# Attention probabilities stored with 128 columns per head and group, so that each weight load begins on a 256-byte boundary of its tile

## The chip, the cores and the metric

The kernel runs on one core of one Trainium2 chip. The metric is the device time of one execution in microseconds (us), as the median of several. TensorE (PE in the profile) multiplies a stationary operand, its weights, by a moving operand that streams through it. Each matmul here has its own weight load, which the profile lists as a separate engine, PEld. DVE is VectorE, ACT is ScalarE, POOL is GpSimd. All profiles quoted here had a granted TensorE clock of 1.00.

## The reference, cut to what matters

The reference has two halves, a state-space layer and a segmented attention with a small memory. The change touches the attention alone.

```python
# 64 segments of 32 rows, 8 memory rows in front; 32 heads of 128; x is 2048 x 1024
h = jnp.concatenate([mem, xs], axis=1)
q, k, v = (jnp.einsum('btd,dhe->bhte', h, W) for W in (Wq, Wk, Wv))   # shortened
scores = jnp.where(mask, jnp.einsum('bhqe,bhke->bhqk', q, k) * scale, -1e9)
p = softmax(scores)
o = jnp.einsum('bhqk,bhke->bhqe', p, v)
o = jnp.einsum('bhte,hed->btd', o, Wo)
mem = o[:, :8]                                   # goes to the next segment
```

## The kernel before

The segments are packed into 22 groups of 96 rows plus 3 memory rows, 99 in all (`GW`). A unit is two groups by two heads, and there are 16 head pairs with 11 units each, so 176 units. For each unit TensorE computes four transposed score blocks (99 columns each), ScalarE takes their exponentials into `b_e`, GpSimd multiplies by a 0/1 mask into `b_m`, and two units later TensorE uses `b_m` as the weights of four matmuls. Their moving operand is the value tile `b_v`. It has 258 columns per group: a column of ones, the values of two heads, and another column of ones, so the row sum comes out with each product.

```python
GX = 96; GW = 99; VW = 258
...
        for i in range(2):
            t = pool.tile([128, NG, VW], BF16, name=f"b_v{i}", bufs=1)
            G.memset(t[GX:128, :, :], 1.0)
            G.memset(t[:, :, 0:1], 1.0)
            G.memset(t[:, :, VW - 1:VW], 1.0)
            self.vb.append(t)
        for i in range(4):
            t = pool.tile([128, 4 * GW + 32], BF16, name=f"b_m{i}", bufs=1)
            G.memset(t[GX:128, :], 0.0)
            G.memset(t[:, 4 * GW:4 * GW + 32], 0.0)
            self.mb.append(t)
...
    def att_front(self, hp, u):                      # scores, exponential, mask
        ...
                PE.matmul(s[:, j * GW:(j + 1) * GW], kt[:, hh, g0:g0 + 128], qt[:, hh, g0:g0 + GW], start=True, stop=True)
        e = self.p3.tile([GW, 4 * GW], BF16, name="b_e", bufs=3)
        k.S.activation(e[:], s[0:GW, 0:4 * GW], ACT.Exp, scale=float(E) ** -0.5, accum_out=...)
        m = self.mb[i % 4]
        k.G.tensor_tensor(v4(m[0:GW, 0:4 * GW]), v4(e[:]), mask[...], ALU.mult)
...
    def att_back(self, hp, u, m):                    # probabilities times values
        vt = self.vb[hp % 2]
        o = k.ps("O")
        for gg in range(2):
            for hh in range(2):
                j = 2 * gg + hh
                cs = slice(hh * 129, hh * 129 + 129)
                PE.matmul(o[:, gg, cs], m[:, j * GW:j * GW + 128], vt[:, 2 * u + gg, cs], start=True, stop=True)
        ...                                          # reciprocal of the row sums, scaling, store
```

In what follows, positions 0 to 3 are the four matmuls of a unit in the order in which they run (j = 0 to 3). In this kernel their weight loads begin 0, 198, 396 and 594 bytes into `b_m`, and their moving operands begin at 0, 258, 516 and 774 bytes of a stretch of `b_v`.

Of the kernel before, what the change touches and what calls it, by code (L numbers as in the profile page):

```python
# [9 lines left out]
BF16 = mybir.dt.bfloat16  # L10
I32 = mybir.dt.int32
ACT = mybir.ActivationFunctionType
ALU = mybir.AluOpType
# [303 lines left out]
class PartB:  # L317
# [201 lines left out]
    def qk_init(self, pool):  # L519
        V, G = self.k.V, self.k.G  # L520
        self.qk = []
        for i in range(2):
            pair = []
            for n in "qk":
                t = pool.tile([128, 2, QW], BF16, name=f"b_{n}{i}", bufs=1)
                V.memset(t[:, :, 64 + NMX:GX], 0.0)
                V.memset(t[:, :, 21 * GW + 64:21 * GW + GX], 0.0)
                V.memset(t[:, :, NG * GW:QW], 0.0)
                pair.append(t)
            self.qk.append(pair)  # L530
        self.vmst = []
        for i in range(2):
            t = pool.tile([128, 4, 128], BF16, name=f"b_vmst{i}", bufs=1)
            V.memset(t[:, :, NM:128], 0.0)
            self.vmst.append(t)
        self.vb, self.mb = [], []
# [4 lines that stand above are left out]
            G.memset(t[:, :, VW - 1:VW], 1.0)  # L541
            self.vb.append(t)
        for i in range(4):
            t = pool.tile([128, 4 * GW + 32], BF16, name=f"b_m{i}", bufs=1)
            G.memset(t[GX:128, :], 0.0)
            G.memset(t[:, 4 * GW:4 * GW + 32], 0.0)
            self.mb.append(t)

    def load_wqk(self, hp):
# [55 lines left out]
    def att_front(self, hp, u):  # L605
        k = self.k; PE = k.PE
        qt, kt = self.qk[hp % 2]
        s = k.ps("S")
        for gg in range(2):
            g0 = (2 * u + gg) * GW  # L610
# [4 lines that stand above are left out]
        i = hp * NU + u  # L615
        k.S.activation(e[:], s[0:GW, 0:4 * GW], ACT.Exp, scale=float(E) ** -0.5, accum_out=self.accE[0:GW, i:i + 1])  # L616
        m = self.mb[i % 4]
        mask = k.maskA if u == 0 else k.maskB
        v4 = lambda t: t.rearrange("p (a b q) -> p a b q", a=2, b=2)
        k.G.tensor_tensor(v4(m[0:GW, 0:4 * GW]), v4(e[:]), mask[0:GW, :, :].unsqueeze(2).to_broadcast([GW, 2, 2, GW]), ALU.mult)  # L620
        return m

    def att_back(self, hp, u, m):
        k = self.k; PE, V = k.PE, k.V
# [3 lines that stand above are left out]
            for hh in range(2):  # L628
                j = 2 * gg + hh
                cs = slice(hh * 129, hh * 129 + 129)  # L630
                PE.matmul(o[:, gg, cs], m[:, j * GW:j * GW + 128], vt[:, 2 * u + gg, cs], start=True, stop=True)  # L631
        i = hp * NU + u
        r = self.rall[0:GW, 4 * i:4 * i + 4]
        oa = o[0:GW]
        ends = bass.AP(oa.tensor, oa.offset, [list(oa.ap[0]), [512, 2], [257, 2]])
        V.reciprocal(r.rearrange("p (a b) -> p a b", a=2), ends)  # L636
        ot = self.ot[hp]
        V.tensor_tensor(ot[:, 2 * u:2 * u + 2, :].rearrange("p g (h e) -> p g h e", h=2),  # L638
                        oa[:, :, 1:257].rearrange("p g (h e) -> p g h e", h=2),
                        r.rearrange("p (a b) -> p a b", a=2).unsqueeze(3).to_broadcast([GW, 2, 2, E]), ALU.mult)  # L640
        if u == NU - 1:
            os = self.os[hp // 4]
            cs = slice((hp % 4) * 256, (hp % 4) * 256 + 256)
            k.SP.dma_start(os[64:64 + 20 * GX, cs].rearrange("(g p) n -> p g n", p=GX), ot[0:GX, 1:21, :])
            k.SP.dma_start(os[0:64, cs], ot[0:64, 0, :])
            k.SP.dma_start(os[T - 64:T, cs], ot[0:64, 21, :])
            cs = slice(hp * 256, hp * 256 + 256)
            k.SP.dma_start(self.omd[0:NTL, cs].rearrange("(g j) n -> j g n", j=3), ot[GX:GW, :, :])
            k.SP.dma_start(self.omd[NTL:NM, cs], ot[64:64 + NMX, 0, :])
# [489 lines left out]
```

## Time and profile before

| | before |
|---|---|
| time, median of the first 3 runs | 1241.64 us (1241.46 to 1241.79) |
| PE busy, of a span of 1240.4 us | 1230.1 us |
| PE busy in the attention stage, 497 to 1017 us | 519.84 of 520 us |
| weight loads from `b_m`, of all weight loads | 704 of 8148 |

Three lines of the page, kernel before: the busy times by engine, and from the list of groups the matmuls on the probabilities and the largest group of matmuls. The columns of a group are line, engine, operation, output and inputs, shape, count, then busy us with the mean ns of one, then idle time before.

```profile
PE 1230.1 (99%) x8078; PEld 654.6 (53%) x8148; DVE 610.7 (49%) x1124; ACT 326.0 (26%) x754; POOL 211.6 (17%) x290
...
L587 PE MATMUL psP<-b_xe,w 128*128 128x480 bf16 x2048 | 439.3, 366 | 0.0
...
L631 PE MATMUL psO<-b_v,b_m 128*128 128x129 bf16 x704 | 70.0, 221 | 0.0
```

TensorE is the bound. L631 shows a trap: 70.0 us over 704 matmuls are 99 ns each, which for 129 columns looks far too long. But a matmul's end is modelled in this profile, and the recorded time of one (221 ns) reaches well over the start of the next. What a matmul costs in a stream is the time from its start to the next start, here called its pitch. Starts are in the timeline, here of TensorE's matmuls in one unit of the kernel before (start in us, recorded length, then the group):

```profile
599.76 1.90 PE L570 MATMUL psP<-b_xe,w 128*128 128x201 bf16 x20
601.49 0.34 PE L613 MATMUL psS<-b_q,b_k 128*128 128x99 bf16 x4
601.67 0.40 PE L631 MATMUL psO<-b_v,b_m 128*128 128x129 bf16 x4
601.91 1.38 PE L587 MATMUL psP<-b_xe,w 128*128 128x480 bf16 x6
```

The four score matmuls (L613) take from 601.49 to 601.67, which is 45 ns each, and the four on the probabilities (L631) from 601.67 to 601.91, 60 ns each. The starts recorded in the whole trace give means of 56.9, 60.3, 59.3 and 59.4 ns for positions 0 to 3, 58.96 ns over all. (One gap in this trace, of 275 ns, spans a missing record and is left out.)

The view of tile `b_m`, kernel before: each group's count, then minimum, median and maximum ns of one, first and last start.

```profile
L631 PEld LDWEIGHTS <-b_m x704: 97/98/100, 502.3 to 1016.7; 128*128 128x128 bf16 x176
L620 POOL TENSOR_TENSOR b_m<-b_e,maskB x160: 869/871/876, 499.8 to 1015.3; 99x396 bf16<-99x396 bf16 x160
...
  ACT b_e L616: 383.7, 176
```

All 704 loads are recorded at 97 to 100 ns, the aligned ones of position 0 as well as the others. The last line says that GpSimd sat idle for 383.7 us, in 176 waits, for the exponentials. From the end of a unit's multiply to its first load pass 3.8 us in the median, but less in the last head pair: 0.7 us in most of its units, and 0.18 us in the last.

### The profile page before, as it was taken

What the parts mean: (1) busy time and instruction counts of PE and PEld (TensorE: products, weight loads), DVE (VectorE), ACT (ScalarE), POOL (GpSimd) and SP (SyncE); (2) the same over time, 40 slices, a digit from 0 to 9 for tenths busy, and PEclk for the clock granted to TensorE, in tenths of its full rate; (3) what the DMA queues carried; (4) which work ended last, traced back from release to release, by engine and by line L of the source; (5) the groups of instructions that cost most, each with busy time, mean ns of one, the idle gap of its engine ahead of it and who ended that gap; (6) DMA issues with size and microseconds to landing.
All of it is one profiled execution on the core that took longest, in us unless ns stands there. A gap on an engine that the chain in (4) does not pass through costs nothing.

```text
span 1240.4 us, 19648 instructions
## 1 busy us (share of the span) xinstructions
PE 1230.1 (99%) x8078; PEld 654.6 (53%) x8148; DVE 610.7 (49%) x1124; ACT 326.0 (26%) x754; POOL 211.6 (17%) x290
## 2 busy tenths in 40 slices
PE   8999999999999999999999999999999999999998
PEld 4444444444455445566666655655565554454444
DVE  4889999999941122444444444444444550011000
ACT  3344334444310001332333333333333230000000
POOL 2000000000032144222222222232222330000000
PEclk9999999999999999999999999999999999999999
DMA  9942232333666558577668554645575469707000
GB/s 220 261 132 66 87 94 68 102 94 77 153 187 203 154 166 164 106 151 149 134 128 170 124 136 96 128 77 104 106 139 106 73 203 218 153 18 153 17 18 28
DMA packets 306056, 153.95 MB, mean 124 GB/s; under 512 B 147242, under 2 KB 299810, under 8 KB 305962
## 3 DMA queue, kind: packets, MB, share of 16 engines
q1 hardware_dynamic: 304138, 150.82, 52.6%
q10 hardware_dynamic: 1824, 1.84, 0.5%
q8 instruction: 65, 1.06, 0.4%
q14 instruction: 29, 0.24, 0.1%
HBM read 73.70 MB, written 44.71 MB: 95 GB/s over the span
## 4 chain that ended last, share of the span: by engine, by line
PE 98%; DMA 1%; issue 0%; DVE 0%
PE psP L587 33%; PE psS L687 9%; PE psO L256 9%; PE psS L414 9%; PE psP L414 9%; PE psP L687 5%; PE psP L310 4%; PE psS L310 4%; PE psP L570 4%; PE psO L631 3%; PE psS L613 3%; PE psO L687 2%; PE psS L720 1%; PE psP L505 1%; PE psP L739 1%; DMA a_hs<-in_B_Wv_dram 1%
## 5 line engine op out<-in xcount | busy, mean ns | idle before, releaser
L587 PE MATMUL psP<-b_xe,w 128*128 128x480 bf16 x2048 | 439.3, 366 | 0.0
L587 PEld LDWEIGHTS <-w 128*128 128x128 bf16 x2048 | 193.9, 98 | 183.0
L620 POOL TENSOR_TENSOR b_m<-b_e,maskB 99x396 bf16<-99x396 bf16 x160 | 139.4, 871 | 347.5 <-ACT b_e L616 347.5
L77 DVE CAST b_q<-psP 128x480 bf16<-128x480 f32 (+1 forms) x192 | 98.0, 531 | 145.3 <-PE psP L587 133.8
L414 PEld LDWEIGHTS <-b_xe 128*128 128x128 bf16 x1024 | 99.8, 98 | 121.7 <-DMA a_hs<-in_B_Wv_dram 1.1
L75 ACT ACTIVATE b_k<-psP 128x480 bf16<-128x480 f32 x128 | 73.1, 571 | 318.7 <-PE psP L587 318.7
L687 PEld LDWEIGHTS <-b_ol 128*128 128x128 bf16 x960 | 93.1, 98 | 109.3
L616 ACT ACTIVATE b_e<-psS 99x396 bf16<-99x396 f32 x176 | 87.4, 497 | 170.5 <-PE psS L613 161.7
L638 DVE TENSOR_TENSOR b_ot<-psO,b_rall 99x512 bf16<-99x512 f32 x176 | 121.6, 691 | 6.4
L256 PE MATMUL psO<-w,a_bt 128*128 128x512 bf16 x496 | 114.7, 379 | 0.8
L636 DVE RECIPROCAL b_rall<-psO 99x4 f32<-99x4 f32 x176 | 31.1, 177 | 132.5 <-PE psO L631 132.5
L687 PE MATMUL psS<-w,b_ol 128*128 128x512 bf16 x406 | 91.5, 379 | 0.6
L414 PE MATMUL psS<-w,b_xe 128*128 128x512 bf16 x378 | 90.1, 379 | 0.4
L414 PE MATMUL psP<-w,b_xe 128*128 128x512 bf16 x376 | 89.8, 379 | 0.4
L256 PEld LDWEIGHTS <-a_bt 128*128 128x128 bf16 x512 | 49.7, 98 | 59.0
L310 PEld LDWEIGHTS <-a_hs 128*128 128x128 bf16 x512 | 49.5, 98 | 58.3
L77 DVE CAST b_ost<-psS 128x512 bf16<-128x512 f32 x13 | 9.0, 691 | 125.4 <-PE psS L687 125.4
L631 PE MATMUL psO<-b_v,b_m 128*128 128x129 bf16 x704 | 70.0, 221 | 0.0
L613 PEld LDWEIGHTS <-b_k 128*128 128x128 bf16 x704 | 50.0, 98 | 33.9 <-DVE b_k L77 0.2
L613 PE MATMUL psS<-b_q,b_k 128*128 128x99 bf16 x704 | 60.1, 208 | 0.1
L75 ACT ACTIVATE b_vst<-psS 128x512 bf16<-128x512 f32 x56 | 33.4, 597 | 99.1 <-PE psS L414 70.2
L353 POOL MEMSET b_z<- 32x128 bf16 x1 | 0.2, 194 | 341.3 <-DVE a_hs L292 341.3
(205 smaller groups left out, 1162.3 us busy)
## 6 DMA issues: line engine op xcount, KB each, us to landing
b_v<-b_vx SPq DMA_DIRECT2D x16, 1056.0 KB
b_os<-b_ot SPq DMA_DIRECT2D x16, 960.0 KB
w<-in_B_Wv_dram SPq DMA_DIRECT2D x14, 1024.0 KB
b_vx<-b_vst SPq DMA_DIRECT2D x48, 256.0 KB
w<-in_B_Wo_dram SPq DMA_DIRECT2D x12, 1024.0 KB
w<-in_B_Wq_dram SPq DMA_DIRECT2D x16, 512.0 KB
w<-in_B_Wk_dram SPq DMA_DIRECT2D x16, 512.0 KB
a_xn<-in_A_x_dram SPq DMA_DIRECT2D x32, 128.0 KB
```

The costliest lines, as they stand in the source:

```text
L75: self.S.activation(out, in_, ACT.Copy)
L77: self.V.tensor_copy(out, in_)
L256: m = PE.matmul(u[:, i, :], self.bt[:, i, c, :], self.xT[tb][:, c, :], start=(c == 0), stop=(c == KC - 1))
L310: PE.matmul(py[:], self.hs[tb][:, pc, i, tt * 128:(tt + 1) * 128], self.ct[half, i][:, pc, :], start=(pc == 0 and i == 0), stop=(pc == PC ...
L414: m = self.k.PE.matmul(p[:], self.xe[:, c, t * 128:(t + 1) * 128], w[:, c, :], start=(c == 0), stop=(c == KC - 1))
L587: PE.matmul(p[:, 0:480], w[:, i * KC + c, hh * 128:(hh + 1) * 128], self.xe[:, c, 480 * q:480 * q + 480], start=(c == 0), stop=(c == KC - 1))
L613: PE.matmul(s[:, j * GW:(j + 1) * GW], kt[:, hh, g0:g0 + 128], qt[:, hh, g0:g0 + GW], start=True, stop=True)
L616: k.S.activation(e[:], s[0:GW, 0:4 * GW], ACT.Exp, scale=float(E) ** -0.5, accum_out=self.accE[0:GW, i:i + 1])
L620: k.G.tensor_tensor(v4(m[0:GW, 0:4 * GW]), v4(e[:]), mask[0:GW, :, :].unsqueeze(2).to_broadcast([GW, 2, 2, GW]), ALU.mult)
L631: PE.matmul(o[:, gg, cs], m[:, j * GW:j * GW + 128], vt[:, 2 * u + gg, cs], start=True, stop=True)
L638: V.tensor_tensor(ot[:, 2 * u:2 * u + 2, :].rearrange("p g (h e) -> p g h e", h=2), oa[:, :, 1:257].rearrange("p g (h e) -> p g h e", h=2) ...
L687: k.PE.matmul(self.acc[t, half], ol[:, h8, tt * 128:(tt + 1) * 128], self.wo_half(half, h), start=(h == 0), stop=(h == H - 1))
```

## The change

The intent: in the old tile only position 0 loads its weights from the start of the tile, and the other loads begin at odd multiples of 2 bytes and 4 bytes. If a load that begins off a boundary is slower, then 528 loads would gain. The new tile gives each head and group 128 columns (256 bytes). The added columns hold zeros, as the tile is cleared once and only 99 columns of each block are ever written again.

```diff
         for i in range(4):
-            t = pool.tile([128, 4 * GW + 32], BF16, name=f"b_m{i}", bufs=1)
-            G.memset(t[GX:128, :], 0.0)
-            G.memset(t[:, 4 * GW:4 * GW + 32], 0.0)
+            t = pool.tile([128, 4, 128], BF16, name=f"b_m{i}", bufs=1)
+            G.memset(t[:], 0.0)
             self.mb.append(t)
@@ att_front
-        k.G.tensor_tensor(v4(m[0:GW, 0:4 * GW]), v4(e[:]), mask[0:GW, :, :].unsqueeze(2).to_broadcast([GW, 2, 2, GW]), ALU.mult)
+        k.G.tensor_tensor(m[0:GW, :, 0:GW].rearrange("p (a b) q -> p a b q", a=2), v4(e[:]), mask[0:GW, :, :].unsqueeze(2).to_broadcast([GW, 2, 2, GW]), ALU.mult)
@@ att_back
-                PE.matmul(o[:, gg, cs], m[:, j * GW:j * GW + 128], vt[:, 2 * u + gg, cs], start=True, stop=True)
+                PE.matmul(o[:, gg, cs], m[:, j, :], vt[:, 2 * u + gg, cs], start=True, stop=True)
```

The built program keeps the order of all instructions but for four memsets. It places the new tiles 128 bytes past a multiple of 256 (read from the built program), so the boundary is a true one of 128 bytes, and of 256 only within the tile. The changed kernel is one line shorter there, so its L630, L619 and L586 are the L631, L620 and L587 of before.

## The prediction

> What bounds the kernel. TensorE: the page's first part has PE busy 1230.1 of 1240.4 us, and the chain that ended last is 98% PE. In the attention stage (497 to 1017 us) the windows view has PE busy 519.84 of 520 us at a granted clock of 1.00. The change gains only what it takes off PE's own pitch.
>
> What it touches. 704 of 8148 weight loads (those from b_m, four per unit, 176 units) and the GpSimd multiply that writes b_m. The order of instructions on PE, DVE, ACT and SP stays; GpSimd loses four memsets. The old tile's loads begin at 0, 198, 396 and 594 bytes, the new one's at 0, 256, 512, 768. In the built program the new tile begins 128 bytes past a multiple of 256, so loads are aligned to 128 bytes only. Tiles below in the pool move by 640 bytes.
>
> Cost. The group list invites a wrong sum: L631 has 70.0 us for 704 matmuls, 99 ns each, where 129 columns should stream in about 56; 43 ns x 704 would be 30 us. But matmul ends are modelled. Read by starts: in the timeline the four score matmuls start at 601.49, the four b_m matmuls at 601.67, the next projection at 601.91: 45 ns per score matmul (99 columns), 60 per b_m matmul. Over all units, start to start is 44 to 45 ns for L613; for L631 it averages 56.9 after a unit's first matmul, then 60.3, 59.3 and 59 to 60: mean 59.0. The 480-column matmuls have 202.4. A line through 99 and 480 columns gives 56.5 ns at 129 (estimate). All above streaming is thus 2.5 ns x 704 = 1.8 us, 0.14% of the run.
>
> Is even that alignment? I think mostly not. The Trainium skill (TensorE: Matmul & The Clock Gate, Part 2, step 1) says the next weights load while the current matmul runs; the trace agrees: each load starts 2 ns after a matmul starts. The score matmuls load b_k at steps of 198 bytes, just as unaligned, at a pitch of 44 to 45 ns: an unaligned load fits into that and cannot hold up a matmul that streams for 56. A b_m load's record is 97 to 100 ns, aligned or not. The page's section on weight-path perf modes gives as conditions of the fast load 128 weights, not FP32, a bounded column step; no start address. And the slow gaps follow the matmul's own position, also where its successor's weights are aligned; every fourth unit is slow in position 0 too, where only the value operand's address differs. That points to the moving operand (258-byte steps), which stays.
>
> GpSimd. The multiply takes 871 ns; with rows of 99 in a stride of 128 I expect 870 to 950. It idles 384 us waiting for the exponentials, and PE takes b_m about two units (6 us) later: nothing reaches PE.
>
> Prediction: 1241.0 us, range 1239.3 to 1242.4; faster by over 2% 0.01, within 2% 0.98, slower 0.01.
>
> What shows it. Right: L631 starts still about 59 ns apart after positions 1 to 3, loads still 98 ns, PE never waiting for b_m. If alignment mattered, positions 1 to 3 fall to 56 to 57 and the time to about 1239.9. Wrong: a load that costs PE time outside its group, a GpSimd write slow enough to stall PE (over 2.5 us), or the shifted addresses of b_q, b_k, b_v changing other matmuls' pitch.

## The result

| | runs | median us | range us |
|---|---|---|---|
| before | 6 | 1241.76 | 1241.46 to 1242.03 |
| changed | 6 | 1241.76 | 1241.15 to 1242.52 |

The ratio is 1.000, with a 95% interval of 0.9987 to 1.0013: the same. (A ratio is the mean time of one kernel's runs over that of the other's of the same rounds, so not quite the ratio of the medians.)

The same views of the changed kernel: page, timeline of one unit, and tile `b_m`.

```profile
PE 1230.2 (99%) x8078; PEld 654.9 (53%) x8148; DVE 610.8 (49%) x1124; ACT 326.4 (26%) x754; POOL 211.8 (17%) x286
...
L586 PE MATMUL psP<-b_xe,w 128*128 128x480 bf16 x2048 | 439.3, 366 | 0.0
...
L630 PE MATMUL psO<-b_v,b_m 128*128 128x129 bf16 x704 | 69.9, 221 | 0.0
```

```profile
600.78 0.34 PE L612 MATMUL psS<-b_q,b_k 128*128 128x99 bf16 x4
600.97 0.40 PE L630 MATMUL psO<-b_v,b_m 128*128 128x129 bf16 x4
601.20 1.98 PE L586 MATMUL psP<-b_xe,w 128*128 128x480 bf16 x9
```

```profile
L630 PEld LDWEIGHTS <-b_m x704: 96/98/101, 501.6 to 1016.0; 128*128 128x128 bf16 x176
L619 POOL TENSOR_TENSOR b_m<-b_e,maskB x160: 872/874/878, 499.2 to 1014.6; 99x396 bf16<-99x396 bf16 x160
...
  ACT b_e L615: 384.0, 176
```

Nothing that the change aims at has moved. The loads are recorded at 98 ns as before, four matmuls take 0.23 to 0.24 us as before, and the multiply costs 874 ns instead of 871, on an engine that still idles 384 us.

The profiled run of the changed kernel is 0.7 us shorter (1239.7 against 1240.4), and it is worth seeing where. From the start of the span to the first matmul on the probabilities it took 501.69 us against 502.38. From the first of those matmuls to the last it took 514.32 against 514.36. From there to the start of the kernel's last matmul it was 219.85 in both. So the 0.7 us came before the first matmul that the change touches. Two later traces with the aligned tile spent 502.29 and 502.73 us there, so this is scatter from run to run. The middle stretch, called the stretch below, is far more steady than the run time, and is used as the fine measure: four traces, of the kernel before, the changed kernel, a second run of it, and e2_base256 below, have 514.36, 514.32, 514.32 and 514.32 us.

### The profile page after: what moved, and what is told of

Read it like the earlier page. It is cut to its first block, busy times and chain, and to the rows that moved or that the text cites. A ratio compares the mean times of both kernels' runs of the same rounds, so it can differ in the third digit from the quotient of the medians.

```text
span 1239.7 us, 19648 instructions
## 1 busy us (share of the span) xinstructions
PE 1230.2 (99%) x8078; PEld 654.9 (53%) x8148; DVE 610.8 (49%) x1124; ACT 326.4 (26%) x754; POOL 211.8 (17%) x286
## 4 chain that ended last, share of the span: by engine, by line
PE 98%; DMA 1%; issue 0%; DVE 0%
PE psP L586 33%; PE psS L686 9%; PE psO L256 9%; PE psS L414 9%; PE psP L414 9%; PE psP L686 5%; PE psP L310 4%; PE psS L310 4%; PE psP L569 4%; PE psO L630 3%; PE psS L612 3%; PE psO L686 2%; PE psS L719 1%; PE psP L505 1%; PE psP L738 1%; PE psO L482 1%
## 5 line engine op out<-in xcount | busy, mean ns | idle before, releaser
L586 PE MATMUL psP<-b_xe,w 128*128 128x480 bf16 x2048 | 439.3, 366 | 0.0
L586 PEld LDWEIGHTS <-w 128*128 128x128 bf16 x2048 | 193.9, 98 | 183.0
L619 POOL TENSOR_TENSOR b_m<-b_e,maskB 99x396 bf16<-99x396 bf16 x160 | 139.9, 875 | 346.8 <-ACT b_e L615 346.8
L310 PEld LDWEIGHTS <-a_hs 128*128 128x128 bf16 x512 | 49.5, 98 | 58.3
L630 PE MATMUL psO<-b_v,b_m 128*128 128x129 bf16 x704 | 69.9, 221 | 0.0
L612 PE MATMUL psS<-b_q,b_k 128*128 128x99 bf16 x704 | 60.1, 208 | 0.1
```

Source lines behind the costliest of these rows:

```text
L310: PE.matmul(py[:], self.hs[tb][:, pc, i, tt * 128:(tt + 1) * 128], self.ct[half, i][:, pc, :], start=(pc == 0 and i == 0), stop=(pc == PC ...
L586: PE.matmul(p[:, 0:480], w[:, i * KC + c, hh * 128:(hh + 1) * 128], self.xe[:, c, 480 * q:480 * q + 480], start=(c == 0), stop=(c == KC - 1))
L619: k.G.tensor_tensor(m[0:GW, :, 0:GW].rearrange("p (a b) q -> p a b q", a=2), v4(e[:]), mask[0:GW, :, :].unsqueeze(2).to_broadcast([GW, 2, ...
L630: PE.matmul(o[:, gg, cs], m[:, j, :], vt[:, 2 * u + gg, cs], start=True, stop=True)
```

## The experiments

The theory: where a weight load begins does not matter here, since the loads run under the streaming of the matmul before. The 2 to 4 ns above streaming in positions 1 to 3 belong to the moving operand. Rival A: unaligned loads are slower, and this is those 2 to 4 ns, or it is hidden. Rival B: only a true 256-byte boundary helps, and the new tile is 128 bytes off it.

### Loads with nothing to hide under (e1_probe)

In one unit of every head pair, 12 sets of 8 extra matmuls are put in front of the real ones. They write to the same PSUM tile, so that the result stays correct.

```diff
         o = k.ps("O")
+        if u == 5:
+            mf = m[:].rearrange("p a q -> p (a q)")
+            W = lambda off, r: mf[:, off + 128 * (r % 2):off + 128 * (r % 2) + 128]
+            v = vt[:].rearrange("p g n -> p (g n)")
+            b0 = 8 * VW
+            for r in range(8):
+                PE.matmul(o[:, 0, 0:32], W(0, r), v[:, b0:b0 + 32], start=True, stop=True)
+            ...   # the same with W(64, r), W(1, r), W(2, r), W(32, r), W(99, r)
+            ...   # six sets of 128 or 129 columns, one operand moved at a time
```

> The changed kernel with 96 extra matmuls in one unit of every head pair (16 units), eight in a row for each of twelve settings, written to a PSUM tile that the real matmuls then overwrite. Six settings have 32 columns, so that the weight load and not the streaming sets the pitch: loads beginning 0, 128, 2, 4, 64 and 198 bytes into the tile (the tile itself begins 128 bytes past a multiple of 256, so the second alone is on a 256-byte boundary). Six have 128 or 129 columns and change one operand at a time: weights at 0 or 198 bytes, value operand at 0 or 258 bytes, output at column 0 or 129. Theory (a load's start does not matter): the six short settings have one pitch within 1 ns, somewhere from 25 to 40 ns, and 129 columns stay at 56 to 57 ns with weights at 0 and at 198 bytes; the 59 to 60 ns appear with the value operand at 258 bytes or the output at column 129. Rival A (an unaligned load is slower but hidden): the settings at 2, 4, 64 and 198 bytes are at least 3 ns longer than that at 0. Rival B (only a true 256-byte boundary helps): the setting at 128 bytes is alone the fastest by at least 3 ns.

The timeline of TensorE's matmuls in one such unit; L632 to L642 are the six sets of 32 columns, L644 and L646 have 129 columns with the loads at 0 and at 198 bytes:

```profile
556.81 0.35 PE L632 MATMUL psO<-b_v,b_m 128*128 128x32 bf16 x8
557.01 0.35 PE L634 MATMUL psO<-b_v,b_m 128*128 128x32 bf16 x8
557.21 0.35 PE L636 MATMUL psO<-b_v,b_m 128*128 128x32 bf16 x8
557.41 0.35 PE L638 MATMUL psO<-b_v,b_m 128*128 128x32 bf16 x8
557.61 0.35 PE L640 MATMUL psO<-b_v,b_m 128*128 128x32 bf16 x8
557.81 0.35 PE L642 MATMUL psO<-b_v,b_m 128*128 128x32 bf16 x8
558.01 0.61 PE L644 MATMUL psO<-b_v,b_m 128*128 128x129 bf16 x8
558.46 0.62 PE L646 MATMUL psO<-b_v,b_m 128*128 128x129 bf16 x8
558.92 0.62 PE L648 MATMUL psO<-b_v,b_m 128*128 128x129 bf16 x8
```

Each set of eight takes 0.20 us, 25 ns per load and matmul, wherever the load begins. Over all 16 units the gaps within five of the six sets are 25 ns without one exception, 112 each. The first set has 25.6, because its first gap, right after the score matmuls, is mostly 28. The Trainium skill (TensorE: Matmul & The Clock Gate, Part 1, "Wait — 56ns, not 53.3ns?") gives about 25 ns as a floor of the distance between starts, however few the columns, and this trace agrees. So a load whose true cost is below 25 ns would not show, and whether the start matters below that stays open. Here it cannot matter: the shortest pitch in attention that an unaligned load must fit into is 44 ns. With 129 columns the means are 56.3 and 56.7 ns for loads at 0 and 198 bytes; the 0.4 ns are not the load's start, as a set of the second probe has 56.7 with the loads at 0. Rivals A and B both fall.

The expectation about the moving operand held only in part. With the moving operand kept at 258 bytes (L648) only the first gap of each set is 61 ns, and then it settles at 56 to 58. With the output at column 129 it is 56.8. So what costs is neither place by itself; it appears when the moving operand changes. That led to the second probe.

### A true 256-byte boundary (e2_base256)

```diff
             self.mb.append(t)
+        pad = pool.tile([128, 64], BF16, name="b_pad", bufs=1)
+        G.memset(pad[:], 0.0)
```

> The changed kernel with a pad of 128 bytes after the four tiles, so that every load of the probabilities begins on a true multiple of 256 bytes. Theory (start does not matter): same time, ratio to the kernel before 0.999 to 1.001, starts after positions 1 to 3 still 59 to 61 ns apart. Rival B (only the true boundary helps): positions 1 to 3 fall to 56 to 57 ns, the time by 1.5 to 2 us (ratio about 0.9985).

The built program has the tiles at multiples of 256 bytes. The time is 1241.22 us in the median of 5 runs against 1242.07 of 9 runs before; the ratio is 0.9993 (0.998 to 1.0007), the same. The ratio alone could not exclude the 1.5 us of rival B, but the trace does: the positions have 56.9, 60.3, 59.2 and 59.3 ns, and the stretch is 514.32 us.

### Twice the loads, half the cover (e3_split_after, e4_split_before)

```diff
-                PE.matmul(o[:, gg, cs], m[:, j, :], vt[:, 2 * u + gg, cs], start=True, stop=True)
+                for c in (slice(hh * 129, hh * 129 + 65), slice(hh * 129 + 65, hh * 129 + 129)):
+                    PE.matmul(o[:, gg, c], m[:, j, :], vt[:, 2 * u + gg, c], start=True, stop=True)
```

The second kernel makes the same edit to the kernel before.

> The changed kernel with every matmul on the probabilities cut in two (65 and 64 columns), so that each load is made twice and has half the streaming time to hide under: 704 loads more, pitch near 30 ns by streaming (estimate from the slope between 99 and 480 columns). Theory: if streaming or a fixed load time sets the pitch, both this and the cut version of the kernel before come out equal within 1 us, at 0 to 15 us above the kernel before. Rival A: this one is faster than the cut kernel before by at least 3 us (3 ns on 1056 unaligned loads).

> The kernel before with the same cut (65 and 64 columns), its loads at 0, 198, 396 and 594 bytes. Theory: the same time as the cut version of the changed kernel within 1 us, and the same pitch by position. Rival A: at least 3 us longer, with the pitch of positions 1 to 3 longer than that of position 0.

| | median us | ratio to before | mean pitch ns | stretch us |
|---|---|---|---|---|
| cut, aligned loads | 1246.40 | 1.0035 (1.0019 to 1.005) | 32.0 | 517.98 |
| cut, loads at 198-byte steps | 1246.06 | 1.0031 (1.0015 to 1.0046) | 32.1 | 518.09 |

Doubling the loads costs 3.7 us of stretch in both. With 32 ns of room instead of 59, the aligned loads gain 0.1 us in the stretch, which is 0.1 ns for each of the 1056 loads, and their kernel is not faster by the clock. Rival A asked for 3 us.

### What the 2 to 4 ns are (e6_probe2)

A second probe of the same form, all with 128 or 129 columns, moves one thing between a matmul and the next.

```diff
+            for r in range(8):
+                PE.matmul(o[:, 0, 0:129], W(0, r), v[:, B + 129 * (r % 2):B + 129 * (r % 2) + 129], start=True, stop=True)
+            ...   # and eleven other sets; two of them are the real pattern of four:
+                PE.matmul(o[:, r % 4 // 2, ...], mf[:, 128 * (r % 4):128 * (r % 4) + 128], v[:, B + 129 * (r % 4):...], ...)
+                PE.matmul(o[:, r % 4 // 2, ...], mf[:, 99 * (r % 4):99 * (r % 4) + 128], v[:, B + 129 * (r % 4):...], ...)
```

> What the 2 to 4 ns above streaming in positions 0 to 3 come from. The changed kernel with 96 extra matmuls in one unit of every head pair, eight in a row for each of twelve settings, overwritten by the real ones. All have 129 columns but two with 128. Settings: nothing changes between matmuls; the value operand alternates between 0 and 258 bytes; the output alternates between columns 0 and 129; both alternate; both alternate with 128 columns (256 bytes, column 128); the value operand alternates by 1032, by 288 and by 260 bytes; the output alternates between two banks; the real pattern of four with the loads at 0, 256, 512, 768 bytes; the real pattern with the loads at 0, 198, 396, 594 bytes; the real pattern with 128 columns. Theory (moving operand): nothing changing gives 56 to 57 ns, the value operand alternating by 258 bytes gives 59 to 61 ns by itself, the output alternating by itself stays at 56 to 57. Rival C (the output's place): the other way round. On the change itself: the real pattern has the same pitch, position by position within 1 ns, with aligned and with unaligned loads; if an unaligned load cost anything under these matmuls, the second is longer in positions 1 to 3.

Seven of the sets in one such unit, in the timeline: L632 is the set in which nothing moves, L634 has the moving operand alternate by 258 bytes, L636 the output, L638 both. L650 and L652 are the real pattern with aligned and with unaligned loads, L654 that with 128 columns. L659 are the real matmuls of the unit.

```profile
519.06 0.62 PE L632 MATMUL psO<-b_v,b_m 128*128 128x129 bf16 x8
519.51 0.63 PE L634 MATMUL psO<-b_v,b_m 128*128 128x129 bf16 x8
519.98 0.61 PE L636 MATMUL psO<-b_v,b_m 128*128 128x129 bf16 x8
520.43 0.62 PE L638 MATMUL psO<-b_v,b_m 128*128 128x129 bf16 x8
...
523.16 0.63 PE L650 MATMUL psO<-b_v,b_m 128*128 128x129 bf16 x8
523.63 0.63 PE L652 MATMUL psO<-b_v,b_m 128*128 128x129 bf16 x8
524.10 0.61 PE L654 MATMUL psO<-b_v,b_m 128*128 128x128 bf16 x8
524.54 0.40 PE L659 MATMUL psO<-b_v,b_m 128*128 128x129 bf16 x4
```

From start to start the eight take 0.45 us in L632 and in L636, 0.47 in L634, 0.47 in both L650 and L652, and 0.44 in L654. Median pitches by place in the set, from the starts in the trace:

| set | pitch ns |
|---|---|
| nothing moves | 57 throughout |
| output alternates between columns 0 and 129 | 56 to 57 |
| output alternates between two banks | 56 to 57 |
| moving operand alternates by 258 bytes | 56 to 57 after the one at 0, 60 to 61 after the one at 258 |
| by 260 bytes | 56 to 57, and 59 to 61 |
| by 1032 bytes | 56 to 57, and 56 to 59, unsteady |
| by 288 bytes | 56 to 57 throughout |
| moving operand (258 bytes) and output alternate | 56 to 57, and 59 to 61 |
| moving operand and output alternate, 128 columns (256 bytes) | 55 to 56 throughout |
| real pattern, loads at 0, 256, 512, 768 bytes | 57, 61, 59, 59, 56, 59, 59, 59 |
| real pattern, loads at 0, 198, 396, 594 bytes | 56, 59, 59, 60, 56, 59, 59, 59 |
| real pattern, 128 columns | 55 to 56 throughout |

The last rows but one compare the two tiles side by side in one execution: aligned loads are not faster. One place (the second) differs by 2 ns, in favour of the unaligned ones, and the same place in the second round of four has 59 in both. The excess follows the moving operand alone. The table also says more than the theory did. At 258 bytes a matmul begins exactly where the one before stopped reading (129 columns of 2 bytes). Suppose that the operand is read in lines, blocks of a fixed size. At 260 it then begins in the line in which the one before ended; at 288 and, with 128 columns, at 256, in a fresh line. Lines of 8, 16 or 32 bytes all fit these sets; the texts on record take 32. So two forms of the theory are left: the start off a multiple of 32 bytes costs, or the start in the line in which the stream before ended. The first probe's trace already leans to the second form. Its set L648 begins at 258 bytes after a stream that ended at 257, and its first pitch is 60.9 ns in the mean of 16 sets. L654 begins at the same 258 bytes after a stream of 128 columns that ended at 255, and its first pitch is 56.6 ns.

### The moving operand aligned, with and without aligned loads (e7_moving_before, e8_moving_after)

```diff
-VW = 258
+VW = 272
-            G.memset(t[:, :, VW - 1:VW], 1.0)
+            G.memset(t[:, :, 257:258], 1.0)
-        for i in range(4):
+        for i in range(3):                       # the buffers of b_m, for space; also i % 3
-                cs = slice(hh * 129, hh * 129 + 129)
-                PE.matmul(o[:, gg, cs], m[...], vt[:, 2 * u + gg, cs], ...)
+                cs = slice(hh * 129, hh * 130 + 129)
+                PE.matmul(o[:, gg, cs], m[...], vt[:, 2 * u + gg, hh * 128:hh * 129 + 129], ...)
# and the columns that the reciprocal and the scaling read
```

> The kernel before with its loads left at 0, 198, 396 and 594 bytes and only the value operand moved: the rows of the value tile are 544 bytes apart instead of 516, the second head of a group is read from 256 bytes on (130 columns, the first of them unused) and written to columns 129 to 258, so every value operand starts a multiple of 32 bytes from its tile's start. Three instead of four buffers of probabilities pay for the space. Theory (the value operand's start makes the 59 to 61 ns): all four positions fall to 55.5 to 57.5 ns, mean 56.5, with unaligned loads; the time falls by 1 to 2 us, ratio to the kernel before 0.9984 to 0.9993. Rival A (unaligned loads cost the 3 ns): positions 1 to 3 stay at 59 or more and the time stays within 0.5 us.

> The changed kernel with the same edit to the value operand. Theory: the same pitch and time as the same edit of the kernel before, within 0.5 us, so that the aligned loads add nothing to it. Rival A: this one alone falls to 56 to 57 ns in positions 1 to 3, and is at least 1 us faster than the other.

> The changed kernel itself once more, beside the two others on one chip. Theory: within 0.5 us of the kernel before, and 1 to 2 us slower than the two with the value operand aligned.

| | median us | ratio to before | pitch in positions 0 to 3, ns | stretch us |
|---|---|---|---|---|
| before with moving operand aligned | 1241.35 | 0.9997 (0.9984 to 1.0011) | 56.5, 60.6, 55.8, 60.2 | 513.90 |
| changed with moving operand aligned | 1241.37 | 0.9997 (0.9984 to 1.0011) | 56.5, 60.6, 55.8, 60.1 | 513.90 |
| changed, once more (e9_after_again) | 1241.67 | 1.0000 (0.9987 to 1.0014) | 56.9, 60.3, 59.2, 59.3 | 514.32 |

Half of the theory came out. Position 2, which now begins on a fresh row, fell from 59.3 to 55.8 ns, with unaligned loads as well as with aligned ones. Position 0 of every fourth unit (units 3 and 7 of a head pair, where it begins 24 bytes past a multiple of 32 in the tile) had stood at 59 ns and fell to 57. But positions 1 and 3 stayed at 60, though they begin at a multiple of 32 bytes. What they still do is to begin at byte 256 of a row whose first 258 bytes the matmul before has just read: in the line in which it ended. The expected 1 to 2 us was 0.46 us of stretch, and by the clock the changed kernel run beside them was only 0.3 us slower than the two.

### The heads in the other order (e10_swap_before, e11_swap_after)

If the line that is read twice in a row is the cost, then no layout is needed, only another order.

```diff
     def att_back(self, hp, u, m):
         for gg in range(2):
-            for hh in range(2):
+            for hh in (1, 0):
```

> The kernel before with the two heads of a group multiplied in the other order (second, then first), nothing else: loads at 198, 0, 594, 396 bytes, value operands at the same misaligned starts, but no value operand starts any more where the one before it ended. Theory (a value operand that starts in the 32-byte line in which the one before it ended costs 3 to 4 ns): all four positions fall to 55.5 to 57.5 ns but perhaps in every fourth unit, and the stretch from the first to the last of these matmuls shrinks from 514.3 us by 1.2 to 1.8 us. Rival D (a start that is no multiple of 32 bytes costs it, whatever came before): three positions stay at 59 to 61 ns and the stretch stays within 0.3 us. Rival A (unaligned loads): the slow positions are those with the loads at 198, 396 and 594 bytes, now the first, third and fourth.

> The changed kernel with the same swap. Theory: the same pitch and the same stretch as the swapped kernel before, within 0.2 us; aligned loads add nothing. Rival A: shorter than the swapped kernel before by at least 1 us.

One unit in the timeline of the swapped kernel before:

```profile
601.46 0.34 PE L613 MATMUL psS<-b_q,b_k 128*128 128x99 bf16 x4
601.64 0.39 PE L631 MATMUL psO<-b_v,b_m 128*128 128x129 bf16 x4
601.86 1.38 PE L587 MATMUL psP<-b_xe,w 128*128 128x480 bf16 x6
```

The four matmuls now take 0.22 us instead of 0.24. Over the trace, in the order in which they run:

| | median us | ratio to before | pitch, first to fourth, ns | stretch us |
|---|---|---|---|---|
| swapped, loads at 198, 0, 594, 396 bytes | 1240.88 | 0.9994 (0.998 to 1.0007) | 56.9, 56.3, 58.3, 56.0 | 513.05 |
| swapped, loads at 256, 0, 768, 512 bytes | 1240.35 | 0.9986 (0.9973 to 1.0) | 56.9, 56.3, 58.3, 56.0 | 513.04 |

Three of four positions are at the streaming time, though three of four moving operands still begin off a 32-byte multiple: rival D falls as the main cause. The mean pitch went from 58.96 to 56.88 ns, and the stretch lost 1.31 us, 0.1% of the run. (704 pitches would give 1.46 us; the rest went to the 480-column matmuls, 202.44 instead of 202.37 ns each.) The two rows are equal to 0.01 us of stretch, with aligned loads and without. By the medians the swap is 1.0 and 1.5 us faster than the kernel before in the same rounds (1241.86 us), but the intervals still reach 1.0, so only the traces show it.

What is left depends on the start within 32 bytes, and a start off a multiple is not always slow. The first position is at 59 ns only in units 3 and 7 (26 bytes past a multiple of 32). The third is at 58, 60, 58 and 56 ns where it begins 6, 14, 22 and 30 bytes past one. The fourth stays at 56 to 57 at 4, 12, 20 and 28.

### Both edits (e12_swap_rows)

This is the aligned moving operand of the kernel before (above) with the swapped order.

```diff
 # on top of VW = 272 and the second head at 256 bytes
-            for hh in range(2):
+            for hh in (1, 0):
```

> The kernel before with both edits of the value operand: rows 544 bytes apart with the second head from 256 bytes on, and the second head multiplied first. The loads stay at 0, 198, 396 and 594 bytes. Theory (what is left at 58 to 60 ns in one position of the swapped kernel is a value operand's start off a 32-byte multiple): every position of every unit at 55 to 57.5 ns, the stretch from the first to the last of these matmuls 512.5 to 512.9 us. If the remainder has another cause, one position stays at 58 or more and the stretch at 513.0 us. If unaligned loads cost anything here, the positions with loads at 198, 396, 594 bytes stay above 58.

It missed its mark. The pitches are 56.4, 57.1, 56.8 and 57.6 ns and the stretch is 513.26 us, slightly longer than with the swap alone. The slow position fell as expected (58.3 to 56.8), but the first and third matmuls have one more column, the second and fourth rose by 0.8 and 1.6 ns, and the 480-column matmuls stood at 202.50 ns. The time is 1240.65 us, ratio 0.999 (0.9977 to 1.0004). So where the stream starts does count for something in the third position and in every fourth unit, but why the second and fourth positions rise stays open. The simple swap is the version to keep: its traces beat both kernels, at no cost.

## Why the prediction was right

- **The bound and the size of the prize.** The prediction read pitch by starts and not by the busy time of a group, and so allowed 1.8 us at most instead of 30. Measured: the group's busy time is 70.0 and 69.9 us in the two kernels, the mean pitch 58.96 and 58.92 ns. The best reordering reached 56.9 ns, close to the 56.5 that the line through 99 and 480 columns gave. That line takes 44 ns, the median, for the score matmuls; with their mean of 44.7 it gives 57.1 ns, and 1.3 us in place of 1.8 (estimates).
- **An unaligned load costs nothing here.** Shown: 25 ns per load at every start tried (e1_probe), the same pitch in the real pattern with both sets of loads (e6_probe2), and with doubled loads 0.1 us of stretch between the two tiles (e3_split_after, e4_split_before). The 128 bytes by which the new tile misses a true boundary, which the prediction pointed out, made no difference either (e2_base256). The Trainium skill (TensorE: Matmul & The Clock Gate, Part 2, step 1) says that the next weights load while the current matmul runs, and the traces agree: all 704 loads from `b_m` begin 1 or 2 ns after the start of a matmul.
- **The slow positions follow the moving operand.** Right in the operand, too simple in the form. The prediction named its "258-byte steps"; what the runs show is that most of the cost arises when a stream begins in the line in which the stream before it ended. At 258 bytes that is so for every step within a unit. Reordering the two heads removed it without moving any address.
- **GpSimd.** 874 ns were measured where 870 to 950 were expected, and TensorE never waited for it. But the prediction's bound for a stall, 2.5 us, was loose: with 0.2 to 0.7 us from multiply to load in the last head pair, a much smaller delay could have been felt there.
- **The time.** 1241.76 us lies in the range of 1239.3 to 1242.4, but 0.76 us above the forecast of 1241.0. The forecast left room for a small gain from alignment; the stretch shows 0.04 us. The time alone proves little: the range also held 1239.9, the time that the prediction gave for the case that alignment mattered. The pitches tell the two apart.

## What to carry to other kernels

Before you align an operand, ask whether its load is what sets the distance between starts. Read that distance from the timeline, not from the busy time or the recorded length of an instruction; here those suggested 43 ns to gain per matmul, where 2.5 were there. Then compare with a neighbour that already has the suspected fault: the score matmuls loaded weights at 198-byte steps at 44 to 45 ns, and this pointed to the answer before any run. And where consecutive matmuls stream adjacent pieces of one tile, try another order.

## What the Trainium skill lacked or had wrong

- TensorE: Matmul & The Clock Gate, weight-path perf modes: its conditions for a fast weight load name no start address, and it does not say that the start is free. Here 128-column bf16 loads beginning 0, 2, 4, 64, 128 and 198 bytes into a tile all ran at 25 ns from start to start.
- The same page, on LDWEIGHTS, gives the time of a load as its columns over 1.2, in ns (107 for 128 columns). The recorded length is 98 ns, but loads of 128 columns follow each other every 25 ns with 32-column matmuls, so neither figure is what a load costs in a stream.
- The same page, on the back-to-back gap, gives about 81 ns per matmul at 128 columns and 131 at 512 as the sustained rate with a load for each. Here, with a load for each, the pitch was 55 to 56 ns at 128 columns, and 216 ns at 512 (the median in both kernels' traces), which its formula of columns over 2.4 plus 2.5 ns does match.
- No page tells that a moving operand which begins in the line where the one before ended costs 3 to 4 ns (lines of 8, 16 or 32 bytes fit the probe). Here it was 60 to 61 ns instead of 56 at 129 columns, and 1.31 us of stretch over 528 such steps, most of it cured by order alone. What sets the 1 to 4 ns that remain at some starts is open.
- SBUF — State Buffer, operand start alignment, says of its own measurements that they are about legality and timed nothing. For TensorE's two operands the numbers above are a start.
